# Banded and residue-grouped attention tiles, one Mish activation, and an order written by hand: a fused sparse-attention and MLP kernel

## The chip, the cores and the metric

One core of a Trainium2 chip runs the kernel. Its engines work side by side, each with a queue of its own: TensorE (PE; its weight loads are PEld), VectorE (DVE), ScalarE (ACT), GpSimd (POOL) and SyncE (SP, which here only issues DMAs). The metric is the device time of one execution in microseconds, the median of the runs. TensorE's clock is granted at one of two levels, 1.2 or 2.4 GHz; the profile gives it as a share of full speed (0.50 or 1.00).

## The reference

The attention has 8 batches, 8 heads, 576 positions and head size 64. Heads 0 to 3 see only the last 32 positions (a band); heads 4 to 7 see the earlier positions with the same residue modulo 32. The rows of all batches then make 4608 tokens of 512 features for an MLP with 2048 hidden units.

```
scores = scale * np.matmul(q, k.transpose(0, 1, 3, 2))
mask_local = (rel >= 0) & (rel < stride)
mask_strided = (rel >= 0) & (pos[None, :] % stride == pos[:, None] % stride)
attn = np.exp(scores)
attn = attn / (np.sum(attn, axis=-1, keepdims=True) + 1e-09)
h = x @ w_in
sp = np.where(h > 20.0, h, np.log1p(np.exp(np.minimum(h, 20.0))))
g = h * np.tanh(sp)
return (g @ w_out).astype(np.float32)
```

The last steps, h times tanh of softplus of h, are the Mish function.

## The kernel before

Setup loads both weights in float32 and casts them on VectorE. `attention_prep` loads q, k and v of a batch in 128-position tiles with 27 DMAs on SP, casts them to bfloat16 on VectorE and transposes q and k on TensorE (L192, into PSUM `trps`, copied out by L197 and L198). `attention_compute` goes head by head: for each tile of 128 keys a score matmul (L227, into `ps`) over the queries that can see it (up to 256 columns for a local head, all later queries for a strided one), an exponential on ScalarE (L240, into `p`), a mask multiply on GpSimd (L241), and, per tile of 128 queries, value matmuls (L258, into `po`) with a column of ones in `vext` that gives the softmax sum. VectorE takes the reciprocal (L266, L267) and scales (L270, into `xnat`). Five transposing DMAs on SP put `xnat` into `xT_sb`, a ring of 2304 tokens.

The MLP takes blocks of 256 tokens: `mlp_a1` is the first product (L120, 256 columns at a time), a copy of h to SBUF (L127) and Exp over the whole 128x4096 tile (L128); `mlp_a2` is Ln(1 + x) (L133); `mlp_b` is Tanh (L138), the multiply with h (L140), the second product (L145, 512 columns) and the store, issued on GpSimd (L153). The loop over batches issues preparation of the next batch, attention of this one, `mlp_b` of the blocks of the batch before, and `mlp_a1` and `mlp_a2` of the blocks that have become complete. The framework's scheduler orders each engine's queue from this; it mixes matmuls of the second product with the next attention where they are ready.

Of the kernel before, what the change touches and what calls it, by code (L numbers as in the profile page):

```python
# [14 lines left out]


def _build_masks(stride: int):
    j = np.arange(128)[:, None]
    s = np.arange(128)[None, :]
    loc = []  # L20
    for d in range(2):
        r = 128 * d + s - j
        loc.append((r >= 0) & (r < stride))
    strd = []
    for d in range(5):
        r = 128 * d + s - j
        strd.append((r >= 0) & ((r % stride) == 0))
    locm = np.stack(loc, axis=1).astype(np.float32)
    strm = np.stack(strd, axis=1).astype(np.float32)
    return (locm.astype(ml_dtypes.bfloat16), strm.astype(ml_dtypes.bfloat16))  # L30
# [3 lines left out]
def kernel(  # L34
    ctx: ExitStack,
    tc: tile.TileContext,
    q: bass.AP,
    k: bass.AP,
    v: bass.AP,
    moe_w_in: bass.AP,  # L40
    moe_w_out: bass.AP,
    out: bass.AP,
):
    nc = tc.nc
    B, H, S, D = q.shape
    DM = moe_w_in.shape[0]
    DF = moe_w_in.shape[1]
    STRIDE = 32
    NT = B * S
    assert S == 576 and D == 64 and H == 8 and DM == 512 and DF == 2048  # L50

    NQB = 5
    scale = 1.0 / float(np.sqrt(D))

    TBLK = 256
    n_blocks = NT // TBLK
    RING = 2304
    assert NT % TBLK == 0 and RING % S == 0 and RING % TBLK == 0

    locmask_np, strmask_np = _build_masks(STRIDE)  # L60
    locmask_h = nc.inline_tensor(locmask_np, name="locmask")
    strmask_h = nc.inline_tensor(strmask_np, name="strmask")
# [5 lines left out]
    xT_sb = const.tile([128, 4, RING], BF16, name="xT_sb")  # L68
    w_in_bf = const.tile([128, 4, DF], BF16, name="w_in_bf")
    w_out_bf = const.tile([128, 16, DM], BF16, name="w_out_bf")  # L70
    locmask = const.tile([128, 2, 128], BF16, name="locmask_sb")
    strmask = const.tile([128, 5, 128], BF16, name="strmask_sb")
    ident = const.tile([128, 128], BF16, name="ident_sb")

    with tc.tile_pool(name="wstage", bufs=1) as wstage:
        w_in_f = wstage.tile([128, 4, DF], F32, name="w_in_f")
        nc.sync.dma_start(
            w_in_f[:], moe_w_in.rearrange("(cc p) f -> p cc f", p=128)
        )
        w_out_f = wstage.tile([128, 16, DM], F32, name="w_out_f")  # L80
        nc.sync.dma_start(
            w_out_f[:], moe_w_out.rearrange("(fc p) o -> p fc o", p=128)
        )
        for cc in range(4):
            nc.vector.tensor_copy(w_in_bf[:, cc, :], w_in_f[:, cc, :])
        for fh in range(2):
            nc.vector.tensor_copy(
                w_out_bf[:, fh * 8:(fh + 1) * 8, :], w_out_f[:, fh * 8:(fh + 1) * 8, :]
            )
    nc.sync.dma_start(locmask[:], locmask_h.ap())  # L90
    nc.sync.dma_start(strmask[:], strmask_h.ap())
    nc.sync.dma_start(ident[:], ident_h.ap())

    ld_pool = ctx.enter_context(tc.tile_pool(name="ld", bufs=1))
    qk_pool = ctx.enter_context(tc.tile_pool(name="qk", bufs=2))
    v_pool = ctx.enter_context(tc.tile_pool(name="vp", bufs=2))
    xn_pool = ctx.enter_context(tc.tile_pool(name="xn", bufs=2))
    p_pool = ctx.enter_context(tc.tile_pool(name="pp", bufs=9))
    small = ctx.enter_context(tc.tile_pool(name="small", bufs=4))
    hs_pool = ctx.enter_context(tc.tile_pool(name="hs", bufs=3))  # L100
    ut_pool = ctx.enter_context(tc.tile_pool(name="ut", bufs=3))
    g_pool = ctx.enter_context(tc.tile_pool(name="gp", bufs=2))
    o_pool = ctx.enter_context(tc.tile_pool(name="op", bufs=1))
    psum_a = ctx.enter_context(tc.tile_pool(name="psa", bufs=2, space=bass.MemoryType.PSUM))
    psum_t = ctx.enter_context(tc.tile_pool(name="pst", bufs=1, space=bass.MemoryType.PSUM))
    psum_m = ctx.enter_context(tc.tile_pool(name="psm", bufs=2, space=bass.MemoryType.PSUM))

    out_f = out

    def mlp_a1(tb):  # L110
        tok0 = tb * TBLK
        r0 = tok0 % RING
        h_sb = hs_pool.tile([128, 16, TBLK], BF16, tag="h_sb", name="h_sb")
        ut = ut_pool.tile([128, 16, TBLK], BF16, tag="ut", name="ut")
        for fc2 in range(8):
            ps = psum_m.tile([128, 2, TBLK], F32, tag="psh", name="psh", bufs=2)
            for j in range(2):
                fc = fc2 * 2 + j
                for cc in range(4):
                    nc.tensor.matmul(  # L120
                        ps[:, j, :],
                        lhsT=w_in_bf[:, cc, fc * 128:(fc + 1) * 128],
                        rhs=xT_sb[:, cc, r0:r0 + TBLK],
                        start=(cc == 0),
                        stop=(cc == 3),
                    )
            nc.vector.tensor_copy(h_sb[:, fc2 * 2:fc2 * 2 + 2, :], ps[:])  # L127
        nc.scalar.activation(ut[:], h_sb[:], AF.Exp)  # L128
        return (tb, h_sb, ut)

    def mlp_a2(state):
        tb, h_sb, ut = state
        nc.scalar.activation(ut[:], ut[:], AF.Ln, bias=1.0, scale=1.0)  # L133

    def mlp_b(state):
        tb, h_sb, ut = state
        tok0 = tb * TBLK
        nc.scalar.activation(ut[:], ut[:], AF.Tanh)  # L138
# [202 lines left out]
```

## Time and profile before

| | |
|---|---|
| median of 3 runs | 709.84 us (709.54 to 712.85) |
| profiled execution: span, first to last instruction | 708.7 us |
| TensorE busy | 516.8 us, 3138 matmuls |
| ScalarE busy | 349.6 us, 439 instructions |
| VectorE busy | 325.0 us, 844 |
| GpSimd busy | 257.1 us, 374 |
| mean granted clock as recorded | 0.790 |

The page gives the profiled execution by its span only; the runs' times lie about 1 us above it. Busy shares are means over stages with different limits, so the sections below go by stretches: what an engine waited for there, and at which clock TensorE ran.

### The profile page before, as it was taken

The page shows a single profiled execution, that of the slowest core. Times are in us where ns is not written, and L with a number is a line of the kernel's source. Part 1 is how long each engine was busy: PE and PEld are TensorE (multiplying, and loading weights), DVE is VectorE, ACT ScalarE, POOL GpSimd, SP SyncE. Part 2 cuts the span into 40 slices and gives each one's busy share as a digit, 9 for nine tenths or more (in the row PEclk, how much of TensorE's full clock was granted, in tenths as well). Part 3 has the DMA queues.
Part 4 walks back from the last instruction along what each step waited for, and adds up shares of the span by engine and source line. Part 5 has one row for each costly group of instructions (what it writes and reads, how often), then busy time and mean ns, then how long its engine had stood idle before and what let it go on. Part 6 is the DMA issues. An engine that isn't in the chain of part 4 may idle for free.

```text
span 708.7 us, 8853 instructions
## 1 busy us (share of the span) xinstructions
PE 516.8 (73%) x3138; PEld 278.2 (39%) x3168; DVE 325.0 (46%) x844; ACT 349.6 (49%) x439; POOL 257.1 (36%) x374
## 2 busy tenths in 40 slices
PE   0058795799388974889768993889379963999655
PEld 0034373337223551348423471337223551338422
DVE  2265675437443465337643374436342343326431
ACT  0014339533944088425973259423953178424960
POOL 0039722470076304750067402851066304740000
PEclk9999996769656885789986695779755895669888
DMA  8697297408900534024330240012000200012001
GB/s 345 206 213 125 34 195 141 105 1 182 205 4 1 117 81 97 1 61 101 71 93 1 63 97 1 0 38 57 0 1 0 81 13 0 1 43 52 0 30 60
DMA packets 139420, 51.70 MB, mean 73 GB/s; under 512 B 134256, under 2 KB 134512, under 8 KB 138864
## 3 DMA queue, kind: packets, MB, share of 16 engines
q1 hardware_dynamic: 136784, 41.70, 27.5%
q0 software_dynamic: 2592, 9.44, 3.6%
q8 instruction: 25, 0.41, 0.3%
q14 instruction: 19, 0.16, 0.1%
HBM read 36.96 MB, written 9.44 MB: 65 GB/s over the span
## 4 chain that ended last, share of the span: by engine, by line
PE 42%; issue 17%; ACT 16%; POOL 13%; DMA 5%; DVE 4%; SPq 3%; POOLq 0%; ACTq 0%; DVEq 0%
PE pso L145 16%; POOL p L241 13%; PE psh L120 10%; PE ps L227 8%; PE po L258 7%; ACT ut L128 5%; ACT ut L133 5%; DMA w_out_f<-in_moe_w_out_dram 3%; ACT p L240 3%; SPq L164 2%; PE trps L192 1%; ACT L133 1%; DMA k<-in_k_dram 1%; ACT L240 1%; ACT L128 1%
## 5 line engine op out<-in xcount | busy, mean ns | idle before, releaser
L240 ACT ACTIVATE p<-ps 128x256 bf16<-128x256 f32 (+4 forms) x352 | 116.5, 365 | 247.8 <-PE ps L227 221.4
L241 POOL TENSOR_TENSOR p<-p,locmask_sb 128x256 bf16<-128x256 bf16 (+2 forms) x160 | 113.2, 727 | 291.6 <-ACT p L240 290.5
L145 PE MATMUL pso<-w_out_bf,gT 128*128 128x512 bf16 x546 | 194.1, 476 | 25.3 <-DVE gT L140 14.9
L241 POOL TENSOR_TENSOR p<-p,strmask_sb 128x512 bf16<-128x512 bf16 (+2 forms) x192 | 130.6, 707 | 51.1 <-ACT p L240 50.8
L227 PE MATMUL ps<-qT,kT 64*128 64x256 bf16 (+4 forms) x352 | 103.2, 341 | 61.3 <-ACT p L240 58.0
L120 PE MATMUL psh<-xT_sb,w_in_bf 128*128 128x256 bf16 x1152 | 134.3, 274 | 0.7 <-DMA xT_sb<-xnat 0.7
L120 PEld LDWEIGHTS <-w_in_bf 128*128 128x128 bf16 x1152 | 112.3, 98 | 21.8 <-issue 1.2
L258 PE MATMUL po<-vext,p 128*128 128x65 bf16 (+2 forms) x768 | 87.9, 233 | 40.9 <-POOL p L241 36.6
L127 DVE CAST h_sb<-psh 128x512 bf16<-128x512 f32 x144 | 99.3, 691 | 30.9 <-PE psh L120 30.5
L128 ACT ACTIVATE ut<-h_sb 128x4096 bf16<-128x4096 bf16 x18 | 65.1, 3615 | 86.5 <-DVE h_sb L127 86.4
L258 PEld LDWEIGHTS <-p 128*128 128x128 bf16 (+2 forms) x768 | 58.4, 120 | 123.1 <-POOL p L241 98.3
L145 PEld LDWEIGHTS <-gT 128*128 128x128 bf16 x576 | 59.6, 111 | 107.0 <-issue 56.6
L266 DVE RECIPROCAL rden<-po 128x4 f32<-128x4 f32 x64 | 11.5, 181 | 163.4 <-PE po L258 162.5
L270 DVE TENSOR_SCALAR xnat<-po,rden 128x64 bf16<-128x64 f32 (+1 forms) x320 | 67.7, 274 | 0.1
L227 PEld LDWEIGHTS <-kT 64*128 64x128 bf16 (+1 forms) x352 | 30.0, 103 | 90.4 <-issue 81.3
L133 ACT ACTIVATE ut<-ut 128x4096 bf16<-128x4096 bf16 x18 | 64.9, 3615 | 0.2
L138 ACT ACTIVATE ut<-ut 128x4096 bf16<-128x4096 bf16 x18 | 64.9, 3610 | 0.0
L140 DVE TENSOR_TENSOR gT<-h_sb,ut 128x4096 bf16<-128x4096 bf16 x18 | 41.2, 2289 | 41.1 <-ACT ut L138 41.1
L152 DVE COPY osb<-pso 128x512 f32<-128x512 f32 x36 | 24.8, 688 | 64.3 <-PE pso L145 63.6
L192 PE MATMUL trps<-ident_sb,qbf 128*128 128x128 bf16 (+1 forms) x160 | 20.1, 247 | 43.4 <-DVE qbf L173 37.1
L153 POOL DMA_DIRECT2D out_dram<-osb x18 | 13.5, 751 | 104.6 <-DVE osb L152 104.6
L192 PEld LDWEIGHTS <-qbf 128*128 128x128 bf16 (+1 forms) x160 | 12.9, 108 | 53.3 <-DVE qbf L173 37.1
(25 smaller groups left out, 179.4 us busy)
## 6 DMA issues: line engine op xcount, KB each, us to landing
q<-in_q_dram SPq DMA_DIRECT2D x72, 128.0 KB, 3.1
k<-in_k_dram SPq DMA_DIRECT2D x72, 128.0 KB, 3.4
v<-in_v_dram SPq DMA_DIRECT2D x72, 128.0 KB, 3.9
out_dram<-osb POOLq DMA_DIRECT2D x18, 512.0 KB, 3.2
w_in_f<-in_moe_w_in_dram SPq DMA_DIRECT2D x1, 4096.0 KB, 12.5
w_out_f<-in_moe_w_out_dram SPq DMA_DIRECT2D x1, 4096.0 KB, 23.2
xT_sb<-xnat SPq DMA_TRANSPOSE x40, 2.4
strmask_sb<-strmask SPq DMA_DIRECT2D x1, 160.0 KB, 9.5
```

The lines of the kernel that those rows point to most:

```text
L120: nc.tensor.matmul(ps[:, j, :], lhsT=w_in_bf[:, cc, fc * 128:(fc + 1) * 128], rhs=xT_sb[:, cc, r0:r0 + TBLK], start=(cc == 0), stop=(cc == 3),
L127: nc.vector.tensor_copy(h_sb[:, fc2 * 2:fc2 * 2 + 2, :], ps[:])
L128: nc.scalar.activation(ut[:], h_sb[:], AF.Exp)
L133: nc.scalar.activation(ut[:], ut[:], AF.Ln, bias=1.0, scale=1.0)
L138: nc.scalar.activation(ut[:], ut[:], AF.Tanh)
L140: nc.vector.tensor_tensor(out=gT[:], in0=h_sb[:], in1=ut[:], op=ALU.mult)
L145: nc.tensor.matmul(po[:], lhsT=gT[:, fc, ot * 128:(ot + 1) * 128], rhs=w_out_bf[:, fc, :], start=(fc == 0), stop=(fc == 15),)
L227: nc.tensor.matmul(ps[0:nk, :], lhsT=kT[pbase:pbase + 64, hp, 128 * kt:128 * kt + nk], rhs=qT[pbase:pbase + 64, hp, sc0:sc0 + ncols], star ...
L240: nc.scalar.activation(pt[0:nk, :], ps[0:nk, :], AF.Exp, scale=scale)
L241: nc.gpsimd.tensor_tensor(out=pt[0:nk, :], in0=pt[0:nk, :], in1=mskap, op=ALU.mult)
L258: nc.tensor.matmul(po_head[0:nq, qb, :], lhsT=pt[0:nk, off:off + nq], rhs=v_ext[0:nk, h, kt, :], start=(ti == 0), stop=(ti == len(kts) - 1),)
L270: nc.vector.tensor_scalar(out=x_nat[0:nq, qb, D * h:D * h + D], in0=po_head[0:nq, qb, 0:D], scalar1=rden[0:nq, qb:qb + 1], scalar2=None, o ...
```

## The change

Nearly the whole kernel function is new. Attention: a local head is cut into six windows of 96 queries by 128 keys (32 before the window and the window); a strided head's positions are regrouped by residue, 7 residues by 18 positions (126 rows) in four tiles and 4 by 18 (72) in a fifth, so that one small tile holds all pairs that the mask allows. Transposed q and k are written in that order by strided copies, v is loaded in that order (26 DMAs on SP per batch), and the result is transposed on TensorE and copied into `xT`, which now holds all 4608 tokens. One score step fills both heads of a pair and several windows, followed by one Exp (L195, L215 or L235) and one or two mask multiplies on GpSimd. MLP: blocks of 512 tokens; the first product (L328) is followed by one Mish activation from PSUM (L333) straight into `gT`; the second product (L343) is as before, its stores on SP. Weights come by GpSimd's DMAs that cast on the way; casts of q, k and v, except the first batch's q and k, go to GpSimd (L124).

The order of every engine's queue is now the program's (`manual_schedule`). During the first product of block t, transposes of batch t+1 follow every second group; during the second product, one list of attention steps of batch t+1 follows each group of four matmuls.

```
+    def cast_qk(b, engs):
+        for src, dst in ((q32, qbf[b % 2]), (k32, kbf[b % 2])):
+            e = next(engs)
+            cast(e, dst[:, 0:2, :, :], src[:, 0:2, :, :])
+            cast(e, dst[:, 2:4, :, :], src[:, 2:4, :, :])
+            cast(e, dst[0:64, 4, :, :], src[0:64, 4, :, :])
...
+        def qk_local(hp, hf):
+            ps = ps_s.tile([128, 2, 512], F32, tag="ps", name="ps")
+            for w in range(3):
+                i = 3 * hf + w
+                for e in range(2):
+                    nc.tensor.matmul(
+                        ps[:, e, WQ * w:WQ * w + WQ],
+                        lhsT=kTl[64 * e:64 * e + 64, hp, WQ * i:WQ * i + 128],
+                        rhs=qTl[64 * e:64 * e + 64, hp, WQ * i:WQ * i + WQ],
+                        start=True, stop=True,
+                    )
+            pt = new_p()
+            nc.scalar.activation(pt[:, :, 0:288], ps[:, :, 0:288], AF.Exp, scale=scale)
+            mk = loc[:, 3 * hf:3 * hf + 3, :].rearrange("p w c -> p (w c)")
+            nc.gpsimd.tensor_tensor(
+                out=pt[:, :, 0:288], in0=pt[:, :, 0:288],
+                in1=mk.unsqueeze(1).to_broadcast([128, 2, 288]), op=ALU.mult,
+            )
...
+        def norm(po, n, dst):
+            rden = small.tile([128, 4], F32, tag="rden", name="rden")
+            nc.vector.reciprocal(rden[0:n, :], po[0:n, :, D])
+            nc.vector.tensor_tensor(
+                out=dst.rearrange("p (h d) -> p h d", h=4), in0=po[0:n, :, 0:D],
+                in1=rden[0:n, :].unsqueeze(2).to_broadcast([n, 4, D]), op=ALU.mult,
+            )
...
+        return [
+            [J(0, 0)], [J(1, 0)], [J(0, 1)], [J(1, 1), W(0)],
+            [Sj(0, 0), W(1)], [Sj(1, 0), W(2)], [Sj(0, 1), W(3)], [Sj(1, 1), W(4)],
+            [qk_str4, W(5)], [lambda: xt_local(0), T(0)], [T(1)], [T(2), lambda: xt_local(1)],
+            [T(3)], [lambda: xt_str((0, 1)), T(4)], [lambda: xt_str((2, 3))],
+            [lambda: xt_str((4,))],
+        ]
...
+            nc.scalar.activation(gT[:, fc, :], ps[:], AF.Mish)
...
+        for t in range(NBLK):
+            gT, g1 = mlp1(t)
+            ts = t_steps(t + 1) if t + 1 < B else []
+            if t + 2 < B:
+                cast_qk(t + 2, forever(nc.gpsimd))
+                cast_v(t + 2, forever(nc.gpsimd))
+            if t + 3 < B:
+                load_qk(t + 3, k32, k)
+                load_qk(t + 3, q32, q)
+                load_v(t + 3)
+            for i, g in enumerate(g1):
+                g()
+                if i % 2 == 1 and i // 2 < len(ts):
+                    ts[i // 2]()
+            at = attn_steps(t + 1) if t + 1 < B else []
+            for i, g in enumerate(mlp2(t, gT)):
+                g()
+                if i < len(at):
+                    for s in at[i]:
+                        s()
```

In the list, J, Sj and qk_str4 are score steps (local, strided, last strided tile), W and T value steps of a local window or a strided tile, xt the transposes of the result. The score tile `ps` and the value tile `po` have one buffer each, `P` six. The loads q32, k32, vl32 and vs32 have one buffer, their casts two.

ScalarE's queue, the activations of two 256-token blocks among the attention's exponentials (`p`), before:

```order
133 L240 ACTIVATE p<-ps 128x256 x3
134 L128 ACTIVATE ut<-h_sb 128x4096
135 L133 ACT_TABLE_LOAD
136 L133 ACTIVATE ut<-ut 128x4096
137 L128 ACT_TABLE_LOAD
138 L128 ACTIVATE ut<-h_sb 128x4096
139 L240 ACTIVATE p<-ps 128x192
140 L133 ACT_TABLE_LOAD
141 L133 ACTIVATE ut<-ut 128x4096
142 L240 ACT_TABLE_LOAD
143 L240 ACTIVATE p<-ps 64x64
```

and now, one 512-token block (L333 is Mish) and the exponentials of the next batch:

```order
11 L333 ACT_TABLE_LOAD
12 L333 ACTIVATE gT<-psh 128x512 x16
13 L195 ACT_TABLE_LOAD
14 L195 ACTIVATE P_84<-ps 128x2x288
15 L195 ACTIVATE P_85<-ps 128x2x288
16 L195 ACTIVATE P_86<-ps 128x2x288
17 L195 ACTIVATE P_81<-ps 128x2x288
18 L215 ACTIVATE P_82<-ps 128x2x252
19 L215 ACTIVATE P_83<-ps 128x2x252
```

Sixteen Mish stand in a run, then one table load, the nine exponentials of a batch (six are shown), and the next load.

TensorE's queue now, in the second product: two groups of local score matmuls (L188) with four matmuls of the second product (L343) between:

```order
527 L188 LDWEIGHTS kTl
528 L188 MATMUL ps<-qTl,kTl 128x96
529 L343 LDWEIGHTS gT
530 L343 MATMUL pso<-w_out,gT 128x512
531 L343 LDWEIGHTS gT
532 L343 MATMUL pso<-w_out,gT 128x512
533 L343 LDWEIGHTS gT
534 L343 MATMUL pso<-w_out,gT 128x512
535 L343 LDWEIGHTS gT
536 L343 MATMUL pso<-w_out,gT 128x512
537 L188 LDWEIGHTS kTl
538 L188 MATMUL ps<-qTl,kTl 128x96
```

The number of 512-column matmuls between two groups of score matmuls is fixed at four; before, it was what the scheduler gave.

GpSimd's queue, before, has masks and stores only:

```order
78 L241 TENSOR_TENSOR p<-p,strmask_sb 128x192
79 L241 TENSOR_TENSOR p<-p,strmask_sb 64x64
80 L241 TENSOR_TENSOR p<-p,locmask_sb 128x256 x2
81 L153 DMA out_dram<-osb 128x2x512
82 L241 TENSOR_TENSOR p<-p,locmask_sb 128x256
```

and now, at block 0, behind the masks of batch 0 (the last is row 26), the casts of batch 1 (to `vs_76`), of batch 2 and then the masks of batch 1:

```order
32 L124 CAST vs_76<-vs_68 128x16x64
33 L124 CAST vs_76<-vs_68 72x4x64
34 L124 CAST qbf_69<-q_65 128x1024 x2
35 L124 CAST qbf_69<-q_65 64x512
36 L124 CAST kbf_71<-k_66 128x1024 x2
37 L124 CAST kbf_71<-k_66 64x512
38 L124 CAST vl_73<-vl_67 128x12x64 x2
39 L124 CAST vs_75<-vs_68 128x16x64
40 L124 CAST vs_75<-vs_68 72x4x64
41 L197 TENSOR_TENSOR P_84<-P_84,loc 128x2x288
```

The casts stand ahead of the next masks in one queue; before, no mask stood behind a cast.

## Rows read from the trace of the kernel before

**Rows 1.** The page, parts 1 and 2: TensorE's busy time, granted clock in 40 slices.
```profile
PE 516.8 (73%) x3138; PEld 278.2 (39%) x3168; DVE 325.0 (46%) x844; ACT 349.6 (49%) x439; POOL 257.1 (36%) x374
...
PEclk9999996769656885789986695779755895669888
```
**Rows 2.** The page, part 4: shares of the chain by engine and by line.
```profile
PE 42%; issue 17%; ACT 16%; POOL 13%; DMA 5%; DVE 4%; SPq 3%; POOLq 0%; ACTq 0%; DVEq 0%
PE pso L145 16%; POOL p L241 13%; PE psh L120 10%; PE ps L227 8%; PE po L258 7%; ACT ut L128 5%; ACT ut L133 5%; DMA w_out_f<-in_moe_w_out_dram 3%; ACT p L240 3%; SPq L164 2%; PE trps L192 1%; ACT L133 1%; DMA k<-in_k_dram 1%; ACT L240 1%; ACT L128 1%
```
**Rows 3.** Groups by line and shape: count, busy us, mean ns, idle before.
```profile
L145 PE MATMUL pso<-w_out_bf,gT 128*128 128x512 bf16 x546 | 194.1, 476 | 25.3 <-DVE gT L140 14.9 <-DVE osb L152 5.1 <-issue 2.9
...
L128 ACT ACTIVATE ut<-h_sb 128x4096 bf16<-128x4096 bf16 x18 | 65.1, 3615 | 86.5 <-DVE h_sb L127 86.4
```
**Rows 4.** Waits: who waited for whom, us in total, times, longest.
```profile
PE ps L227 <- ACT p L240: 58.0, 34, 6.8
...
PE po L258 <- POOL p L241: 36.6, 60, 3.3
```
**Rows 5.** Stretches: length, TensorE busy us (count), granted clock, DMA share, GB/s.
```profile
199.00:213.00 14.00, 14.00 (x52) 0.50 0.00 0
...
224.00:230.00 6.00, 4.45 (x29) 1.00 0.00 0
231.00:237.00 6.00, 5.62 (x24) 0.50 0.26 94
238.00:252.00 14.00, 13.95 (x109) 1.00 0.76 156
...
641.80:661.00 19.20, 19.20 (x171) 1.00 0.09 32
```
**Rows 6.** TensorE in order of time, single stretches: start us, us, instructions.
```profile
37.15 0.77 PE L192 MATMUL trps<-ident_sb,qbf 128*128 128x128 bf16 x5 [37.15 <-DVE qbf L173]
...
340.38 0.52 PE L192 MATMUL trps<-ident_sb,qbf 128*128 128x128 bf16 x5
340.74 0.39 PE L227 MATMUL ps<-qT,kT 64*128 64x192 bf16 x2
...
452.01 0.67 PE L258 MATMUL po<-vext,p 128*128 128x65 bf16 x9
452.62 0.39 PE L145 MATMUL pso<-w_out_bf,gT 128*128 128x512 bf16 x1
...
636.42 3.61 PE L145 MATMUL pso<-w_out_bf,gT 128*128 128x512 bf16 x16 [0.78 <-DVE osb L152]
```
**Rows 7.** Groups by line and shape on GpSimd, ScalarE and VectorE.
```profile
L241 POOL TENSOR_TENSOR p<-p,strmask_sb 128x512 bf16<-128x512 bf16 x32 | 36.8, 1149 | 35.6 <-ACT p L240 35.4
...
L152 DVE COPY osb<-pso 128x512 f32<-128x512 f32 x36 | 24.8, 688 | 64.3 <-PE pso L145 63.6 <-PE ps L227 0.2
...
L240 ACT ACTIVATE p<-ps 128x512 bf16<-128x512 f32 x32 | 19.1, 597 | 43.7 <-PE ps L227 41.0 <-POOL p L241 2.5
L241 POOL TENSOR_TENSOR p<-p,strmask_sb 128x192 bf16<-128x192 bf16 x32 | 18.4, 574 | 0.0
...
L266 DVE RECIPROCAL rden<-po 128x4 f32<-128x4 f32 x64 | 11.5, 181 | 163.4 <-PE po L258 162.5 <-PE ps L227 0.9
...
L173 DVE CAST qbf<-q 128x2048 bf16<-128x2048 f32 x8 | 9.7, 1217 | 6.6 <-DMA q<-in_q_dram 6.6
```
**Rows 8.** ScalarE in order of time at a switch of tables.
```profile
651.62 1.28 ACT L133 ACT_TABLE_LOAD   x1
652.92 3.62 ACT L133 ACTIVATE ut<-ut 128x4096 bf16<-128x4096 bf16 x1
```
**Rows 9.** SP's first loads of q; all engines and DMA from 29 to 62 us.
```profile
29.02 4.23 SPq L164 DMA_DIRECT2D q<-in_q_dram  x8
...
29.00:62.00 33.00, 17.30 (x103) 8.54 (x103) 17.18 (x54) 8.13 (x26) 14.52 (x24) 1.00 1.21 205
```
**Rows 10.** The end in order of time: the last store's issue.
```profile
703.92 0.72 POOL L153 DMA_DIRECT2D out_dram<-osb  x1 [8.07 <-DVE osb L152]
```

More of the change, by code (lines that the diff above doesn't have):

```diff
@@ L67 @@
     const = ctx.enter_context(tc.tile_pool(name="const", bufs=1))
[L68 to L72, printed above, removed]
-    ident = const.tile([128, 128], BF16, name="ident_sb")
[L75 to L86, printed above, removed]
+    w_in = const.tile([128, 4, DF], BF16, name="w_in")
@@ new lines @@
+    NP = 6
+    P = [const.tile([128, 2, 320], BF16, name=f"P{i}") for i in range(NP)]
+    x_l = const.tile([128, NW, 256], BF16, name="x_l")
+    x_s = const.tile([128, NTS, 256], BF16, name="x_s")
+    g_pool = ctx.enter_context(tc.tile_pool(name="gp", bufs=2))
+    small = ctx.enter_context(tc.tile_pool(name="small", bufs=4))
+    o_pool = ctx.enter_context(tc.tile_pool(name="op", bufs=3))
+    PS = bass.MemoryType.PSUM
+    ps_mm = ctx.enter_context(tc.tile_pool(name="psmm", bufs=3, space=PS))
@@ new lines, in cast, with cast_v @@
+    def cast(eng, out_, in_):
+        if eng is nc.scalar:
+            nc.scalar.copy(out_, in_)
+        else:
+            eng.tensor_copy(out_, in_)
+    def cast_qk(b, engs):
[4 more added lines that the diff above has]
+            cast(e, dst[0:64, 4, :, :], src[0:64, 4, :, :])
+    def cast_v(b, engs):
+        for i in range(0, NW, 3):
+            cast(next(engs), vl[b % 2][:, i:i + 3, :, 0:D], vl32[:, i:i + 3, :, :])
+        cast(next(engs), vs[b % 2][:, 0:4, :, 0:D], vs32[:, 0:4, :, :])
+        cast(next(engs), vs[b % 2][0:72, 4, :, 0:D], vs32[0:72, 4, :, :])
@@ new lines, in mlp2, with group @@
+    def mlp2(t, gT):
+        po = {}
+        def group(ot, g4):
+            if g4 == 0:
+                po[ot] = ps_mm.tile([128, 512], F32, tag="mm", name="pso")
+            for fc in range(4 * g4, 4 * g4 + 4):
+                nc.tensor.matmul(
+                    po[ot][:], lhsT=gT[:, fc, 128 * ot:128 * ot + 128], rhs=w_out[:, fc, :],
+                    start=(fc == 0), stop=(fc == 15),
+                )
+            if g4 == 3:
+                osb = o_pool.tile([128, DM], F32, tag="osb", name="osb")
+                nc.vector.tensor_copy(osb[:], po[ot][:])
+                r = 512 * t + 128 * ot
+                nc.sync.dma_start(out[r:r + 128, :], osb[:])
+        return [lambda ot=ot, g4=g4: group(ot, g4) for ot in range(4) for g4 in range(4)]
```

499 lines of the change are left out of this document (257 added, 242 removed).

## The prediction

> **What bounds the kernel now.** I read the page's busy shares first, then the chain, the costliest groups, the waits, and last single stretches in order of time. No engine is full: TensorE is busy 73% of 708.7 us, at a granted clock that swings between its two levels [rows 1]. The chain passes through all of them: TensorE 42%, issue 17%, ScalarE 16%, GpSimd 13% [rows 2]. The reason is alternation. In the attention stage TensorE waits for exponentials (58.0 us in 34 waits) and for GpSimd's masks (36.6 us in 60) [rows 4]; in the MLP stage ScalarE makes three full passes over every 128x4096 tile, 65.1 us and two more rows like it [rows 3], and two of the three passes have 5% of the chain each [rows 2]. The matmuls of the second MLP product show a mean of 476 ns [rows 3], far more than they need, and much of that is the clock: after stretches with idle gaps (224 to 230 us, busy 4.45 of 6 us) the granted clock is 0.50, which is 1.2 GHz, and it stayed there from 199 to 213 us although TensorE was busy all the time; in the dense stretch at 641.8 to 661 us it is 1.00, 2.4 GHz [rows 5]. At 2.4 GHz sixteen 512-column matmuls take 3.61 us; less the 0.39 us of a lone one, 15 intervals of 0.215 us [rows 6].
> One caution for reading: the clock row says 9 for the first slices [rows 1], but five transposes took 0.77 us at 37 us and 0.52 us at 340 us [rows 6]. The start ran at half clock, so before's true mean lies under its 0.79.
>
> **The MLP.** The work is unchanged: 576 matmuls of 512 columns in each product (before, 1152 of 256 in the first). One 512-token block is 128 matmuls by 0.215 = 27.5 us at 2.4 GHz, nine blocks 247.7 us. Gone are the copy of h, the three activations and the multiply with h; table loads remain at two per attention block. In their place comes one Mish from PSUM per 128x512. No row shows Mish. Below, it is one pass like Exp on 128x512 from PSUM, 597 ns; above, as much as three such passes, 1.8 us [rows 7]. I take one pass, since Exp, and the three functions replaced, cost alike per element (3615 ns for 4096) [rows 3]. Against 0.86 us of matmuls per group it is hidden.
>
> **The attention.** A batch becomes 150 small TensorE pieces: 40 transposes of q and k, 22 of the result, 44 score matmuls of 72 to 126 columns, 44 value matmuls of 65. Five transposes at full clock lead the next matmul by 0.36 us (340.38 to 340.74), 72 ns each; nine 65-column matmuls by 0.61 us (452.01 to 452.62), 68 ns [rows 6]. So 106 by 72 and 44 by 68: 10.7 us.
> Masks on GpSimd: 574 ns for 192 columns and 1149 for 512 give 1.8 ns per column over 0.23 us [rows 7]; four of 576 columns (1.26), eight of 252 (0.69), two of 144 (0.49) are 11.5 us per batch. Exponentials: 597 ns for 512 [rows 7], 0.67 in proportion for 576 and 0.60 if nothing were to grow; I take 0.65, and nine make about 5.3 us.
> The f32 to bf16 casts, 7936 columns per batch (2 x 2560 for q and k, 1536 and 1280 for v) in ten instructions, move from VectorE to GpSimd. No row has such a cast on GpSimd: below, VectorE's own (1217 ns for 2048, 0.59 per column); above, GpSimd's two-input rate, 1.8 ns [rows 7]. I take the upper one, the same engine: 16.6 us. GpSimd then works 28 of each block's 41 us, and its casts for batch t+2 run under the first product, ahead of the masks of t+1 in its queue. SP issues 36 loads per batch instead of 27, at 4.23 us for eight [rows 9]: 19 us plus four stores, hidden too.
>
> **Waits in a steady block.** With one score buffer, score matmuls i+1 wait for exponential i. The loop is 0.2 + 0.65 + 0.2 us against 0.86 us of MLP matmuls between; it costs 0.15 us in the two steps without value matmuls. With one output buffer the value matmuls wait for the reciprocal (181 ns) and a 256-column multiply from PSUM, which I put at 0.42, between half and all of the 688 ns copy of 512 [rows 7]: with hand-overs 1.0 us, hidden where score matmuls stand between, 0.15 us in three steps without. At the end of a block the last copy of xT stands on VectorE behind an output copy (0.69): 0.9 us before the first product's third matmul. The table switch before the first exponential stands behind the score matmuls that it waits for, so it shows: 1.28 us with the next activation 0.02 us behind it [rows 8], and TensorE, with 0.86 us to do, stands 1.4 us. Sum 3.2 us (none if the estimates of hand-overs are too long, 6 if each step of the tail waits).
> The Trainium skill (ScalarE: Activation LUTs, What ACT_TABLE_LOAD costs) counts about 1.4 us of drain on top of the load, 2.66 us per switch; this trace shows no such gap. By it seven exposed switches would add 10 us and the time would be 427; by the rows nothing is added.
> A steady block: 27.5 + 10.7 + 3.2 = 41.4 us, as long as GpSimd (28) and SP (22) stay below.
>
> **Start and end.** k and q of batch 0 are 2.36 MB; at 205 GB/s [rows 9] 12 us alone, 23 with as many weight bytes beside them: 18. The 26 issues for v behind them at 0.53 us end at 32, landed 35. GpSimd casts v (5 us), issues four weight loads (0.72 each, as its store [rows 10]), and only then masks: two masks done at 46. Nothing covers this batch: five steps of 1.7 us, five value tiles of 1.45 through the one buffer, and the last transposes end at 62. Block 0 has its own wait: casts for batches 1 and 2 stand on GpSimd before the masks of batch 1, and the last of them waits for v of batch 2, whose issues start when batch 1's v is cast (71 us) and end with landing at 89. Masks from 91, thirteen steps of 1.3: the block ends near 110; I take 108 (97 with casts at 0.59 and k and q at 12; 111 at the other end). Its cover is thin because the loads run one after another at the issue rate, not for want of bandwidth. The end: two blocks without attention, 55.0 us; the last copy, store and completion 5 us, by the 4.8 from the issue of the last store to the end before [rows 10], with 0.9 for the copy ahead of it and less for a store of half the size.
> **Sum:** 108 + 6 x 41.4 + 55 + 5 = 416.4 us of span, against 708.7 in the profiled execution; the median of the runs, 709.84, lies 1.1 above that, so 417. All lower ends together give 97 + 6 x 38.2 + 55 + 4 = 385; all upper ones 111 + 6 x 44.2 + 55 + 6 = 437.
>
> **Rivals.**
> *The clock falls in every attention block.* The 1.4 us at the table switch and the stalls around it could be enough: before, 1.5 us idle in 224 to 230 us preceded a fall, and the half clock then held for 6 us (231 to 237), or 14 and more (199 to 213) under the very mix of 512-column and small matmuls that the change makes everywhere [rows 5]. Against it: here 13.75 of 21.5 us in a second product and 13.75 of 16.6 in a first are full 512-column matmuls, which in 238 to 252 us ran at 1.00. One fall per block with 8 us at half costs 4 us: seven blocks, 28 us, 446. If the whole second product stays at 1.2 GHz (22 us become about 39 in seven blocks): 417 + 119 = 536. The Trainium skill (TensorE: Matmul & The Clock Gate, Part 4) says that transposes do not count as work that frees the clock, which would speak for this case; the transposes at 340 us, at full clock behind dense matmuls [rows 6], do not contradict it, but they do not test it either.
> *GpSimd or the loads bind.* If a cast costs more than 3.8 ns per column, GpSimd's 11.5 + 7936 x that passes 41.4 us and sets the pace. At 5 ns a block is 51 us: 417 + 7 x 10 = 487. **Its extreme is the slower case:** GpSimd would have to need 84 us per batch, ((709 - 60 - 55 - 5)/7), so 9 ns per column, five times its two-input rate [rows 7]. Nothing in the trace points there.
> *Mish is not one pass.* At three passes, 1.8 us per tile, a group is 1.8 instead of 0.86 plus its transposes (0.18 on average): 0.76 us by 144 = 109 us, 526.
> *The start is shorter and the waits are hidden:* 385.
>
> **Chances.** The forecast (392 to 437) 0.55; the clock 0.25, most of it in its smaller form; GpSimd or loads short of the extreme 0.07; Mish 0.04; all better than 392, 0.07; slower than before, by the extreme of casts or what I have not seen, 0.02. The range 392 to 470 leaves out 0.07 below and some 0.12 above. A measurement of this kernel tells about 0.5%, 3.5 us, from no change: faster 0.97, same 0.01, slower 0.02.
>
> **What would show it.** Right: 576 + 576 matmuls of 512 columns at 0.215 us with the clock at 1.00 from about 110 us on; attention blocks of 41 us and two of 27.5; Mish near 0.6 us; casts under 2 ns per column; 1.4 us of TensorE idle before the second group of score matmuls in each block, and nothing of that size elsewhere; the first MLP matmul at 62 us, and a wait of some 7 us for a mask in block 0. Wrong: a clock of 0.50 through second products, GpSimd without idle time, ScalarE releasing first-product matmuls late, or a start much over 110 us.

## The result and the profile after

The changed kernel takes 445.36 us, median of 4 runs (444.04 to 446.55), against 710.42 us for the kernel before on the same chip: a ratio of 0.6265, 95% interval 0.6248 to 0.6282. The forecast was 417 with a range of 392 to 470. The profiled execution has a span of 443.2 us. The page, parts 1, 2 and 4, answering to [rows 1, 2]:

```profile
PE 340.0 (77%) x2352; PEld 160.7 (36%) x2352; DVE 132.8 (30%) x422; ACT 149.6 (34%) x232; POOL 152.1 (34%) x204
...
PEclk9999999995597599999999999999999999999999
...
PE 62%; SPq 22%; DVE 4%; DMA 3%; ACT 3%; POOL 3%; issue 2%; POOLq 0%; ACTq 0%; DVEq 0%
PE psh L328 26%; PE pso L343 24%; SPq L115 13%; SPq L100 6%; PE tr L151 4%; PE po L256 3%; SPq L108 2%; ACT L195 2%; PE po L270 2%; DMA vs<-in_v_dram 1%; PE ps L188 1%; PE ps L208 1%; DMA q<-in_q_dram 1%; POOL P L197 1%; DVE osb L349 1%
```

ScalarE and GpSimd have almost left the chain, with 3% each; TensorE holds 62% of it. What has grown is SP's queue, from 3% to 22%, with the 20 strided loads of v (L115) alone at 13%. The clock row has its low slices between 100 and 155 us (11.1 us a slice) and none behind. Its first 9s mislead here as they did before: at 63.18 us eight matmuls of the first product take 3.61 us, the pace of half clock, where eight take 1.90 us at 191.44.

TensorE in order of time, from block 0 into a steady block (start us, us, instructions, and in brackets the idle time ahead and who ended it):

```profile
63.18 3.61 PE L328 MATMUL psh<-xT,w_in 128*128 128x512 bf16 x8
...
118.09 0.29 PE L256 MATMUL po<-vl,P 128*128 128x65 bf16 x2 [23.80 <-POOL P L197]
...
148.61 2.72 PE L328 MATMUL psh<-xT,w_in 128*128 128x512 bf16 x6 [12.45 <-DVE xT L304]
...
189.69 1.46 PE L328 MATMUL psh<-xT,w_in 128*128 128x512 bf16 x6 [0.38 <-DVE xT L304]
190.98 0.52 PE L151 MATMUL tr<-ident_sb,kbf 128*128 128x128 bf16 x5
191.44 1.90 PE L328 MATMUL psh<-xT,w_in 128*128 128x512 bf16 x8
...
207.72 0.30 PE L188 MATMUL ps<-qTl,kTl 64*128 64x96 bf16 x6
207.96 1.04 PE L343 MATMUL pso<-w_out,gT 128*128 128x512 bf16 x4
210.11 0.30 PE L188 MATMUL ps<-qTl,kTl 64*128 64x96 bf16 x6 [1.11 <-ACT P L195]
...
212.75 0.30 PE L256 MATMUL po<-vl,P 128*128 128x65 bf16 x4
212.89 1.02 PE L343 MATMUL pso<-w_out,gT 128*128 128x512 bf16 x4
213.84 0.29 PE L208 MATMUL ps<-qTs,kTs 64*128 64x126 bf16 x4
...
228.66 1.45 PE L328 MATMUL psh<-xT,w_in 128*128 128x512 bf16 x6 [0.38 <-DVE xT L304]
```

The third matmul of a first product, where TensorE goes on after the wait for `xT`, is a good mark of a block's beginning: 189.69, 228.66, and so on every 38.97 us to 384.52. Inside such a block only two gaps stand out, 1.11 and 0.38 us. Between the first MLP matmul and the first such block there are two long ones, 23.80 and 12.45 us; up to its mark, 148.61, this text counts both to block 0.

GpSimd (casts and masks) and SP (loads and stores) in order of time show what the masks and the stores of block 0 stood behind:

```profile
116.40 0.40 POOL L124 CAST vs<-vs 72x256 bf16<-72x256 f32 x1 [2.02 <-DMA vs<-in_v_dram]
116.77 4.96 POOL L197 TENSOR_TENSOR P<-P,loc 128x576 bf16<-128x576 bf16 x4
```

```profile
0.74 4.16 SPq L100 DMA_DIRECT2D k<-in_k_dram  x5
4.94 16.05 SPq L100 DMA_DIRECT2D q<-in_q_dram  x5
...
26.67 16.25 SPq L115 DMA_DIRECT2D vs<-in_v_dram  x20
...
47.23 17.09 SPq L100 DMA_DIRECT2D q<-in_q_dram  x5
...
84.57 4.17 SPq L100 DMA_DIRECT2D k<-in_k_dram  x5
88.78 5.76 SPq L100 DMA_DIRECT2D q<-in_q_dram  x5
...
98.58 16.22 SPq L115 DMA_DIRECT2D vs<-in_v_dram  x20
...
129.25 16.21 SPq L115 DMA_DIRECT2D vs<-in_v_dram  x20
145.57 3.25 SPq L351 DMA_DIRECT2D out_dram<-osb  x4
```

The loads of batch 2 hold SP from 84.57 to 114.80, its last cast waits for them, and the masks of batch 1 start right behind that cast. SP goes from one load to the next without a gap from 0.74 to 114.80, and that cast begins 1.6 us behind the last issue, so it is SP's queue that sets the time, and not a buffer that comes free late. Then the four stores of block 0 stand on SP behind the loads of batch 3 and issue at 145.57. With three output buffers the fourth copy on VectorE waits for the first store, and the copy of `xT` stands behind it:

```profile
147.77 0.69 DVE L349 COPY osb<-pso 128x512 f32<-128x512 f32 x1 [12.28 <-DMA out_dram<-osb]
```

The groups that answer to [rows 7] (count, busy us, mean ns, idle before):

```profile
L333 ACT ACTIVATE gT<-psh 128x512 bf16<-128x512 f32 x144 | 86.0, 597 | 158.1 <-PE psh L328 158.1
...
L219 POOL TENSOR_TENSOR P<-P,m 128x252 bf16<-128x252 bf16 x64 | 38.9, 637 | 2.2 <-ACT P L215 1.2
...
L124 POOL CAST qbf<-q 128x1024 bf16<-128x1024 f32 x14 | 14.3, 1039 | 17.8 <-DMA q<-in_q_dram 17.8
```

### The profile page after: what moved, and what is told of

It is laid out like the page before. It is cut to its first block, busy times and chain, and to the rows that moved or that the text cites. A ratio compares the mean times of both kernels' runs of the same rounds, so it can differ in the third digit from the quotient of the medians.

```text
span 443.2 us, 6264 instructions
## 1 busy us (share of the span) xinstructions
PE 340.0 (77%) x2352; PEld 160.7 (36%) x2352; DVE 132.8 (30%) x422; ACT 149.6 (34%) x232; POOL 152.1 (34%) x204
## 4 chain that ended last, share of the span: by engine, by line
PE 62%; SPq 22%; DVE 4%; DMA 3%; ACT 3%; POOL 3%; issue 2%; POOLq 0%; ACTq 0%; DVEq 0%
PE psh L328 26%; PE pso L343 24%; SPq L115 13%; SPq L100 6%; PE tr L151 4%; PE po L256 3%; SPq L108 2%; ACT L195 2%; PE po L270 2%; DMA vs<-in_v_dram 1%; PE ps L188 1%; PE ps L208 1%; DMA q<-in_q_dram 1%; POOL P L197 1%; DVE osb L349 1%
## 5 line engine op out<-in xcount | busy, mean ns | idle before, releaser
L328 PE MATMUL psh<-xT,w_in 128*128 128x512 bf16 x576 | 140.7, 391 | 14.8 <-DVE xT L304 14.8
L343 PE MATMUL pso<-w_out,gT 128*128 128x512 bf16 x576 | 144.3, 381 | 0.0
L333 ACT ACTIVATE gT<-psh 128x512 bf16<-128x512 f32 x144 | 86.0, 597 | 158.1 <-PE psh L328 158.1
L197 POOL TENSOR_TENSOR P<-P,loc 128x576 bf16<-128x576 bf16 x32 | 39.8, 1278 | 133.1 <-ACT P L195 133.0
L328 PEld LDWEIGHTS <-w_in 128*128 128x128 bf16 x576 | 52.8, 99 | 75.5 <-issue 22.0
L343 PEld LDWEIGHTS <-gT 128*128 128x128 bf16 x576 | 48.8, 98 | 44.2 <-issue 1.0
L151 PE MATMUL tr<-ident_sb,kbf 128*128 128x128 bf16 (+1 forms) x160 | 18.4, 229 | 28.8 <-DMA ident_sb<-ident 25.3
L215 ACT ACTIVATE P<-ps 128x504 bf16<-128x504 f32 x32 | 18.9, 591 | 63.5 <-PE ps L208 30.6
L219 POOL TENSOR_TENSOR P<-P,m 128x252 bf16<-128x252 bf16 x64 | 38.9, 637 | 2.2 <-ACT P L215 1.2
L195 ACT ACTIVATE P<-ps 128x576 bf16<-128x576 f32 x32 | 20.8, 651 | 42.0 <-PE ps L188 41.9
L124 POOL CAST vs<-vs 128x1024 bf16<-128x1024 f32 (+1 forms) x16 | 11.3, 721 | 48.4 <-DMA vs<-in_v_dram 48.4
L124 POOL CAST qbf<-q 128x1024 bf16<-128x1024 f32 (+1 forms) x21 | 18.1, 896 | 17.8 <-DMA q<-in_q_dram 17.8
L246 DVE TENSOR_TENSOR x_l<-po,rden 96x256 bf16<-96x256 f32 x48 | 20.2, 420 | 1.7
L124 POOL CAST vl<-vl 128x768 bf16<-128x768 f32 x16 | 12.8, 826 | 22.5 <-DMA vl<-in_v_dram 22.5
L124 POOL CAST kbf<-k 128x1024 bf16<-128x1024 f32 (+1 forms) x21 | 18.1, 893 | 0.0
L188 PE MATMUL ps<-qTl,kTl 64*128 64x96 bf16 x192 | 10.2, 213 | 10.0 <-ACT P L195 10.0
```

The source lines that it names most:

```text
L124: eng.tensor_copy(out_, in_)
L151: nc.tensor.transpose(tr[:, 128 * kb:128 * kb + n], src[0:n, kb, 2 * hp:2 * hp + 2, :], ident[0:n, 0:n],)
L195: nc.scalar.activation(pt[:, :, 0:288], ps[:, :, 0:288], AF.Exp, scale=scale)
L197: nc.gpsimd.tensor_tensor(out=pt[:, :, 0:288], in0=pt[:, :, 0:288], in1=mk.unsqueeze(1).to_broadcast([128, 2, 288]), op=ALU.mult,)
L219: nc.gpsimd.tensor_tensor(out=pe, in0=pe, in1=m7.unsqueeze(1).to_broadcast([128, 2, 126]), op=ALU.mult,)
L328: nc.tensor.matmul(ps[:], lhsT=w_in[:, cc, fc * 128:(fc + 1) * 128], rhs=xT[:, cc, 512 * t:512 * t + 512], start=(cc == 0), stop=(cc == 3),)
```

## The experiments

Experiments without another remark start from the changed kernel; the kernel before was run beside each (709.2 to 710.6 us).

### What made the long waits of block 0

**v in natural order.** The strided heads get v's rows in their natural order, so their results belong to other positions; sizes and all other work stay.

```
-            nr = RG if t < 4 else 4
-            for h in range(4):
-                nc.sync.dma_start(
-                    vs32[0:NA * nr, t, h, :],
-                    v[b, 4 + h].rearrange("(a r) d -> a r d", r=32)[:, RG * t:RG * t + nr, :],
-                )
+            n = 126 if t < 4 else 72
+            nc.sync.dma_start(
+                vs32[0:n, t, :, :],
+                v[b, 4:8, 126 * t:126 * t + n, :].rearrange("h p d -> p h d"),
+            )
```

> Left out: the residue grouping of v for heads 4 to 7, which are loaded in their natural order with the same bytes in the same 256-byte pieces, but with 5 issues per batch on SP instead of 20 (their output is then another). Theory A, SP's issue time sets the start (16.2 us of 31 per batch are these 20 issues at 0.81 us): v of batch 0 lands some 12 us earlier, v of batch 2 some 36 us, and the waits of 23.8 us (first mask of batch 1) and 12.4 us (last copy of block 0) go: 395 to 412 us. Theory B, the DMA engines' bandwidth sets it (256-byte pieces beside the weights): the bytes are the same, so 438 to 447 us with both waits still there.

The time is 394.18 us (ratio 0.5543, 0.5513 to 0.5573), just under the range of its theory A. SP in its profile:

```profile
27.56 2.48 SPq L114 DMA_DIRECT2D vs<-in_v_dram  x5
...
95.45 4.22 SPq L350 DMA_DIRECT2D out_dram<-osb  x4
```

As many bytes take 2.48 us of SP in five loads where twenty took 16.25; the stores issue 50 us earlier, and both long waits are gone. The issue of the loads bound block 0, not their bytes. Whether it is the number of issues or their strided pattern was not separated.

**Stores on GpSimd.**

```
-                nc.sync.dma_start(out[r:r + 128, :], osb[:])
+                nc.gpsimd.dma_start(out[r:r + 128, :], osb[:])
```

> The stores go to GpSimd's queue, as before the change. Theory A, the stores of block 0 stand on SP behind the loads of batch 3, and the fourth output copy with the xT copy behind it waits for the first store: the 12.4 us wait at the start of block 1 goes and nothing else does, 431 to 435 us. Rival, the wait comes from the three output buffers and the transfer itself: 443 to 447 us. A second rival: stores between the masks delay GpSimd in each block, over 447 us.

The time is 434.67 us (0.6109, 0.6081 to 0.6136): the 12.45 us are gone, the wait for masks stays at 22.4. The second wait was the stores' place on SP.

**Casts of batch t+2 and loads of batch t+3 behind the second product** instead of ahead of the first.

```
         for t in range(NBLK):
             gT, g1 = mlp1(t)
...
-            if t + 2 < B:
-                cast_qk(t + 2, forever(nc.gpsimd))
-                cast_v(t + 2, forever(nc.gpsimd))
-            if t + 3 < B:
-                load_qk(t + 3, k32, k)
-                load_qk(t + 3, q32, q)
-                load_v(t + 3)
...
             for i, g in enumerate(mlp2(t, gT)):
...
+            if t + 2 < B:
...
+                load_v(t + 3)
```

> The casts of batch t+2 and the loads of batch t+3 are issued behind the second product of block t instead of ahead of the first, so the masks of batch t+1 stand ahead of the casts on GpSimd and the stores ahead of the loads on SP. Theory C, the two late waits of block 0 are a matter of order in the queues: both (23.8 and 12.4 us) go, 405 to 413 us. Theory B, the data are late whatever the order: the wait moves into block 1, where the transposes or masks of batch 2 wait for the same loads, 430 us or more.

The time is 415.06 us (0.5833, 0.5806 to 0.5861). The wait for masks is gone, as expected. The time is over the expected range because the stores still wait: batch 2's loads, issued ahead of the loop, stand before them. TensorE and SP:

```profile
119.74 2.72 PE L328 MATMUL psh<-xT,w_in 128*128 128x512 bf16 x6 [9.12 <-DVE xT L304]
```

```profile
116.70 3.24 SPq L351 DMA_DIRECT2D out_dram<-osb  x4
```

### Can the start be mended?

**w_in issued after the casts of v of batch 0**, so that q and v of batch 0 travel alone.

```
+        cast_v(0, forever(nc.gpsimd))
         for c in range(4):
             nc.gpsimd.dma_start(
                 w_in[:, :, 512 * c:512 * c + 512],
...
-        cast_v(0, forever(nc.gpsimd))
```

> The loads of w_in are issued on GpSimd behind the casts of batch 0's v instead of ahead of them; nothing else. In the changed kernel SP stood at the five loads of q from 4.9 to 21.0 us while w_in moved beside them, and at q of batch 1 from 47 to 64 us beside w_out. If the weights' traffic is what stretches these (each stretch is some 10 us over SP's bare issue time), k and q of batch 0 have landed at 13 to 16 us instead of 25 and the chain of loads behind them on SP moves up by 7 to 10 us: 432 to 438 us. If not (the 256-byte pieces themselves are slow, or the bytes only come later), 441 to 447 us.

The time is 445.46 us (0.6282, 0.6251 to 0.6312): no gain, a miss. SP:

```profile
4.88 5.67 SPq L100 DMA_DIRECT2D q<-in_q_dram  x5
...
36.38 25.70 SPq L100 DMA_DIRECT2D q<-in_q_dram  x5
...
85.29 3.87 SPq L100 DMA_DIRECT2D k<-in_k_dram  x5
```

q of batch 0 is 10 us faster and TensorE begins at 14.58 instead of 25.32, but q of batch 1 now runs beside both weights and takes 25.70. Batch 2's loads begin at 85.29, against 84.57. Block 0 ends when SP has worked through three batches of loads, and that sum did not change.

**Three queues.** Stores on GpSimd, casts behind the second product (both edits above), and v of batch 0 issued on ScalarE's queue.

```
-        load_v(0)
+        load_v(0, nc.scalar)
```

> Casts and loads behind the second product, stores on GpSimd, and the 26 loads of v of batch 0 on ScalarE's queue, which has nothing to do until the first exponential. Theory A and C together (what was lost lies in the order and issue time of the queues): both late waits of block 0 go (about 36 us, of which the late casts alone brought 30), and the 15.9 us wait for the first mask becomes 0 to 5 us: 387 to 397 us. Rival, the loads are as late on any queue because the DMA engines are full: 402 to 410 us.

The time is 430.4 us (0.6073, 0.6041 to 0.6105), another miss, though block 0 is mended: its mark comes at 98.99 instead of 148.61 us. What was lost is in each of the six later blocks with attention, 44.4 to 44.9 us long. GpSimd and TensorE at a block's end:

```profile
99.13 0.54 POOL L351 DMA_DIRECT2D out_dram<-osb  x1 [4.23 <-DVE xT L304]
99.67 2.58 POOL L124 CAST qbf<-q 128x1024 bf16<-128x1024 f32 x3
102.19 2.57 POOL L124 CAST kbf<-k 128x1024 bf16<-128x1024 f32 x3
```

```profile
103.28 0.29 PE L151 MATMUL tr<-ident_sb,kbf 128*128 128x128 bf16 x2 [2.83 <-POOL kbf L124]
```

The casts now stand on GpSimd behind the last store, which waits for the last output copy; the next block's transposes need these casts at once. Either edit alone is harmless, with steady blocks of 38.97 us in both runs above; together they make this wait.

**The same, weights later.** w_in after the casts of v(0), w_out after those of q and k of batch 1.

> As b1, with the loads of w_in behind the casts of v of batch 0 and those of w_out behind the casts of q and k of batch 1. If the weights stretch the first loads, another 5 to 10 us go: 378 to 390 us. If the weights then come too late for the products that need them, no gain over b1 or a loss: 390 to 400 us with a wait of the first or second product of block 0 for a weight load.

The time is 422.43 us (0.5956, 0.5919 to 0.5992): 8 us better, with the same long blocks (44.4 to 44.9 us). It is outside the expected range, so the start alone could not settle the question, and the next two runs test the cast's place.

**Casts and loads at the tenth group of the second product**, behind the batch's last mask and ahead of the last two stores.

```
             for i, g in enumerate(mlp2(t, gT)):
                 g()
...
+                if i == 9:
+                    if t + 2 < B:
+                        cast_qk(t + 2, forever(nc.gpsimd))
...
+                        load_v(t + 3)
```

> The kernel of the run with late weights, with the casts of batch t+2 and the loads of batch t+3 written into the second product at its tenth group: behind the last mask of the batch, ahead of the store issues of the third and fourth token tiles on GpSimd. Theory (the 44.8-us blocks come from casts that stand behind the last store issue on GpSimd): the blocks go back to 39.0 us, the six to seven waits of 2.8 us for kbf and what follows them are gone, and the time is 422 - 6 x 5.8 = 387 us (384 to 394). Rival (the blocks are long for another reason, the moved loads or the stores' own issues on GpSimd): 412 to 425.

The time is 388.57 us (0.5477, 0.546 to 0.5494), as the theory had it. GpSimd in a block:

```profile
85.37 2.57 POOL L124 CAST qbf<-q 128x1024 bf16<-128x1024 f32 x3
...
102.13 1.12 POOL L351 DMA_DIRECT2D out_dram<-osb  x2
```

Now the stores wait for casts, and nobody waits for the stores: block marks at 92.19 and 131.15, 38.96 us apart. This kernel leaves nothing of the work out and is the fastest such kernel here, 57 us under the changed one.

**Only the stores on GpSimd and the casts at the tenth group**, start as in the changed kernel.

> The changed kernel with only two edits: the stores on GpSimd's queue, and the casts of batch t+2 and the loads of batch t+3 at the tenth group of the second product; the loads of the first batches and the weights as in the changed kernel. Theory (both waits of block 0 come from the order in the queues of SP and GpSimd): the 23.8 us and the 12.4 us are gone, block 0 ends at 110 to 114 us, and with six blocks of 39.0, two of 27.5 and an end of 4 the time is 402 to 409 us. Rival (the loads are simply too slow for block 0, whatever the order): a wait of more than 8 us stays in block 0, 414 us or more.

The time is 408.47 us (0.5755, 0.5734 to 0.5777), inside the range. Block 0's mark is at 112.47 us. So the order in the two queues accounts for 37 of the 57 us; v on another queue with the weights later gives the other 20, the two together.

### The steady part, and where the 265 us came from

**No interleave:** all attention steps behind the second product.

```
             for i, g in enumerate(mlp2(t, gT)):
                 g()
-                if i < len(at):
-                    for s in at[i]:
-                        s()
+            for ss in at:
+                for s in ss:
+                    s()
```

> The attention steps of batch t+1 run behind the whole second product of block t, not between its groups of four matmuls; the order of the steps is the same. Theory, the interleave hides the chain of score, exponential, mask and value: batch 0, alone, took 18 us without its mask wait where the steady blocks pay 8 for attention in the second product, and the clock falls in each such stretch: 7 times 10 to 14 us more, 515 to 545 us. Rival, the small tiles alone make attention cheap and the interleave hardly matters: under 465 us.

The time is 532.25 us (0.7481, 0.7431 to 0.753). Windows (length, then busy us and count of TensorE, its weight loads, VectorE, ScalarE, GpSimd; granted clock, DMA share, GB/s):

```profile
240.00:260.00 20.00, 12.95 (x111) 6.95 (x111) 6.64 (x18) 7.93 (x11) 10.65 (x15) 0.80 0.16 57
260.00:280.00 20.00, 17.93 (x109) 9.35 (x112) 6.49 (x25) 6.90 (x12) 7.78 (x10) 0.77 0.90 159
```

Alone, a batch's score and value steps take from 247 to 265 us, and the clock falls in and behind them. The interleave is worth 87 us.

**Mish three times** on each tile (from PSUM, then twice in place), so the output is another.

```
             nc.scalar.activation(gT[:, fc, :], ps[:], AF.Mish)
+            nc.scalar.activation(gT[:, fc, :], gT[:, fc, :], AF.Mish)
+            nc.scalar.activation(gT[:, fc, :], gT[:, fc, :], AF.Mish)
```

> The changed kernel with Mish applied three times to each tile (from PSUM as before, then twice in place), so the output is another; 32 passes more per block on ScalarE, which has some 17 us of work in a steady block. If the work of ScalarE is hidden up to the pace of TensorE and three passes go beyond it, as the prediction's rival has it: a first product takes 16 x 1.8 = 29 us in place of 17, and nine of them (14 in the two pure ones) add 100 us or somewhat less, 520 to 545 us. If ScalarE has more room than that (the second product's time covers the rest): below 480.

The time is 550.02 us (0.7752, 0.7714 to 0.779), a little over the range. A first product is paced by ScalarE, two groups in 3.61 us (313.82 to 317.43), as the rival had it. What it did not count is the block's switch: the exponentials stand behind the last Mish, and TensorE waits 4.67 us there instead of 1.11. In the window behind that wait (columns as above) the clock is at half:

```profile
338.80:344.00 5.20, 5.09 (x30) 1.83 (x31) 0.76 (x2) 1.64 (x3) 3.77 (x3) 0.50 0.02 4
```

```profile
338.78 0.42 PE L188 MATMUL ps<-qTl,kTl 64*128 64x96 bf16 x6 [4.67 <-ACT P L195]
```

This block takes 53.0 us (306.13 to 359.17), its neighbours 51.7 and 52.2.

**The kernel before with Mish alone:** one Mish per 128x512 from PSUM in place of the copy, Exp, Ln, Tanh and the multiply.

```
-            nc.vector.tensor_copy(h_sb[:, fc2 * 2:fc2 * 2 + 2, :], ps[:])
-        nc.scalar.activation(ut[:], h_sb[:], AF.Exp)
...
+            nc.scalar.activation(gT[:, fc2 * 2:fc2 * 2 + 2, :], ps[:], AF.Mish)
...
-        nc.scalar.activation(ut[:], ut[:], AF.Ln, bias=1.0, scale=1.0)
...
-        nc.scalar.activation(ut[:], ut[:], AF.Tanh)
...
-        nc.vector.tensor_tensor(out=gT[:], in0=h_sb[:], in1=ut[:], op=ALU.mult)
```

> One part of the change alone, on the kernel before: one Mish from PSUM to gT for each 128x512 of h in place of the copy of h, Exp, Ln, Tanh and the multiply (gT has four buffers, since it now lives from one batch to the next); attention and order as before. Theory, the stretch of some 21 us per batch in which TensorE waited for ScalarE's passes was the larger part of the loss, and the clock rises with it: 520 to 580 us. Rival, attention's chain of exponentials and masks was the larger part: over 630 us.

The time is 592.63 us (0.836, 0.8272 to 0.8447), between the two expectations. The gain is 117 us. Its ScalarE rows show a new cost:

```profile
L234 ACT ACT_TABLE_LOAD x61 | 78.3, 1283 | 3.7 <-PE ps L221 1.9 <-PEq L319 0.7
L126 ACT ACT_TABLE_LOAD x61 | 78.3, 1283 | 16.8 <-PE psh L119 15.8
```

There the scheduler mixes Mish and Exp, and 122 table loads take 157 us of ScalarE. In the changed kernel sixteen Mish stand together and fifteen switches are left in its queue.

## Why the prediction came out as it did

The direction and the mechanism held, but the point was 28 us low. The 445 us lie above the forecast's own band, 392 to 437; they are inside the range only because it reaches to 470 for the clock rival. That rival's smaller form gave 446 and did not happen, so its nearness is luck. One of the prediction's own signs of being wrong did come, a start much over 110 us. The sum, term by term, with block marks as above:

| | forecast us | measured us |
|---|---|---|
| first MLP matmul | 62 | 63.2 |
| block 0 ends | 108 | 148.6 |
| six steady blocks | 248.4 (41.4 each) | 235.9 (41.1, then five of 38.97) |
| two blocks without attention | 55.0 | 55.0 |
| end | 5 | 3.7 |
| span | 416.4 | 443.2 |

Block 0 was put 40.6 us too short and the six steady blocks 12.5 too long; that the second took back a third of the first is luck too.

**The failed step is "Start and end", block 0.** The prediction had the last cast wait for v of batch 2, let its issues start when v of batch 1 is cast (71 us) and put its landing at 89 us, with loads at 0.53 us each [rows 9]. The mechanism was right: the 23.80 us of wait end with the masks behind that cast, where some 7 us of wait were expected. The size was wrong twice over. The price came from loads of another shape: a k load takes 0.83 us of SP (4.16 for 5), a q load 1.15 with no weights beside it (5.76 for 5), a strided v load 0.81 (16.25 for 20), and a whole batch 30.2 us (84.57 to 114.80), not 19. And beside the weights q took 16.05 and 17.09 us instead of 5.76, which held up the batches behind it; the forecast had slowed batch 0's loads alone. So SP's queue was still at work on the first batches, and v of batch 2 was cast at 116.40. That the issue was to blame, and not the bytes, the run with natural v shows.

**The first MLP matmul, 63.2 against 62,** is close because errors cancelled. The first two masks were done at 50.4 us instead of 46, since v of batch 0 came late (its last cast begins at 44.41, where it was to be done by 40); the rest of batch 0's attention then took 12.8 us instead of 16.

**"19 us plus four stores, hidden too"** is a second miss. In the steady blocks the 31 us are hidden; in block 0 the stores stood behind a batch of loads, and 12.45 us came from a wait that the prediction had not listed. Stores on another queue took it away.

What the prediction called thin cover was seen rightly, but both ends of its bound, 97 to 111 us, used the same price of a load, so the bound could not hold 148.6.

**Steady blocks, 38.97 against 41.4.** The 128 matmuls are as forecast (54.98 us for two blocks). The small pieces cost 8.2 instead of 10.7 us: five transposes lead the next matmul by 0.46 (190.98 to 191.44), 0.09 each instead of 0.072; but six local scores lead by 0.24 (207.72 to 207.96), 40 ns each instead of 72, and four value matmuls by 0.14 (212.75 to 212.89), 35 ns instead of 68. The waits named are 1.11 at the table switch (1.4 forecast) and 0.38 at the block's end (0.9). The remaining 1.8 us are not the steps of 0.15 that were listed but some 0.1 us where a group of four leads to score or value matmuls: 212.89 to 213.84 is 0.95 us, four matmuls need 0.86. Ahead of transposes there is no such step (219.42 to 220.28 is 0.86). All waits together, 3.3 us, come to the 3.2 of the forecast, but by other parts; the gain of the block is that of the small pieces. (The forecast's own parts add up to 10.6 and 3.05, not 10.7 and 3.2, and 417 with 28 is 445, not 446; nothing hangs on that.)

**Mish** is one pass, 597 ns, exactly the Exp of [rows 7]; three passes cost 105 us, where the rival had 109. **Casts** on GpSimd cost 1.0 ns per column, between the bounds of 0.59 and 1.8, about 8.5 us per batch and not 16.6; masks 1278, 637 and 454 ns against 1260, 690 and 490. Had casts cost the upper end, 8 us more, a steady block would probably still have hidden them: GpSimd stands idle for 20.27 us ahead of the first mask at 210.13. No run tried that.

**The table load.** The load takes 1.28 us and the next Exp starts 0.02 us behind it:

```profile
208.11 1.28 ACT L195 ACT_TABLE_LOAD   x1 [1.01 <-PE ps L188]
209.41 0.65 ACT L195 ACTIVATE P<-ps 128x576 bf16<-128x576 f32 x1
```

ScalarE was idle ahead of this load; in the run with three Mish it was not, and there the last Mish ends at 336.77, the load starts at 336.79 and the Exp at 338.08. The Trainium skill (ScalarE: Activation LUTs, What ACT_TABLE_LOAD costs) counts a drain of 1.4 us on top. It shows here no more than in [rows 8]; by it, as an estimate, a switch would stall TensorE for 2.5 us, and it stalls for 1.11.

**The clock rival,** given 0.25, did not happen in steady blocks. Windows of the changed kernel (columns as above):

```profile
118.00:123.00 5.00, 3.97 (x20) 1.41 (x20) 1.20 (x4) 0.59 (x1) 4.29 (x5) 0.56 1.37 214
123.00:135.00 12.00, 11.89 (x111) 5.80 (x111) 8.03 (x28) 3.46 (x5) 11.38 (x18) 1.00 0.88 147
...
148.00:154.00 6.00, 5.39 (x19) 2.15 (x19) 1.12 (x4) 1.65 (x3) 0.00 (x0) 0.57 1.01 228
...
190.00:210.00 20.00, 18.99 (x116) 9.27 (x115) 4.18 (x12) 11.44 (x18) 0.00 (x0) 1.00 0.95 178
210.00:229.00 19.00, 18.41 (x164) 8.52 (x164) 11.22 (x38) 6.07 (x10) 18.55 (x24) 1.00 0.22 66
384.50:439.50 55.00, 54.98 (x254) 24.75 (x253) 4.92 (x8) 19.12 (x32) 0.00 (x0) 1.00 0.10 39
```

Through a whole steady block it is 1.00; behind the two long waits it was mostly at half for 5 to 6 us (0.56, 0.57) and came back under the same mix of matmuls. The second of these stretches is the 2.1 us by which the first of the six blocks is longer. With 4.67 us idle at the switch (three Mish) it fell there as well. So the rival's danger was real; stalls of 1.11 us did not bring it about. In a steady block forty transposes stand among 512-column matmuls and the clock stays at 1.00. They are TensorE's only work just once, for batch 0 from 25.32 to 31 us, where five took 0.77 us instead of 0.52, the pace of half clock. The rule of the Trainium skill (TensorE: Matmul & The Clock Gate, Part 4), that transposes do not free the clock, is not contradicted by either. It is not shown by the second, since that stretch stands behind an idle start and is no longer than those at half behind the long waits.

**Where the 265 us came from** is shown in part. Mish alone took 117 us from the kernel before, in spite of its 122 table loads; undoing the interleave gives back 87. That leaves 60 or so for the attention tiles, the weights' way in, fewer table loads and the rest; which of them has how much was not separated. The two runs start from different kernels, so the parts need not add up.

## What to carry to other kernels

Price a DMA issue by rows of the same shape and count a whole batch's loads on the queue that issues them: where the cover is thin, as in the first block, that queue sets the end, and stores behind it wait too. An instruction that waits late (a store for its last copy, a cast for its last load) holds all that stands behind it on its engine, so ask of each move what it now stands behind; two moves that are harmless alone made a wait of several us per block together. Put what is needed soon ahead of what waits late, as casts ahead of the last stores did.

## What was not expected of the hardware

A strided load of 126 rows of 64 floats (32 KB) holds SP's queue for 0.81 us, longer than a natural-order load of 126 KB, 0.50 to 0.69 us (five, the last of them smaller, took 2.48 for batch 0 and up to 3.43 for the next batches). What makes it so was not tried. The queue also slows with other traffic: the five q loads of the first batches took 5.67 us with no weights beside them, 16 to 17 beside one (16.05 and 17.09), and 25.70 beside both.

Small matmuls came closer to their columns than [rows 6] had led to expect: score matmuls of 96 columns follow each other at 40 ns, which is 96 columns at 2.4 GHz, and value matmuls of 65 at 35 ns, where they took 68 before. Transposes, at 92 ns each (five of them, four with 128 columns and one with 64, in 0.46 us), took longer than the 72 of before. Why the pieces of before were slower was not tried.
